# Turning the convolved blocks once into a staging tile and copying both halves from there, in a convolution and gated-projection kernel

## The chip, the cores and the metric

The kernel runs on one core of one Trainium2 chip. The metric is the device time of one launch in microseconds (us). The engines are named as the profile names them: PE (TensorE, matrix products; PEld is its loading of weights), DVE (VectorE), ACT (ScalarE), POOL (GpSimd) and SP (SyncE). SP computes nothing here. It issues nearly all transfers, in the order of the program, one after the other, and it stands at a semaphore when the next transfer in its order is not yet allowed.

## The reference

Rows of x (8 sequences of 4096 tokens, 192 channels, float32) pass through a causal convolution of 7 taps with softmax weights, one set for each of 8 heads of 24 channels. The result goes through a gated unit:

```python
w = softmax(weight, axis=-1)                       # 8 heads x 7 taps
out = np.einsum('hk,bskhg->bshg', w, x_unf)        # x_unf: the 7 latest tokens, by head
h = x @ w_in                                       # 32768 x 192 @ 192 x 2048
g = h * np.cos(h)
return g @ w_out                                   # 32768 x 2048 @ 2048 x 192
```

## The kernel before

**Units and tiles.** The 32768 tokens are cut into 32 units of U = 1024, each of two tiles of T = 512. For a tile, PE makes the first projection in 8 steps (`mm1`, line 509): a step takes 3 chunks of 64 channels for two groups of 128 output features, as 6 products of 64 rows by 512 tokens into one of three buffers `h` in PSUM. ACT makes the cosine (line 516), DVE multiplies (line 520) into `g`, and PE makes the second projection of the tile before it in 64 steps of two products (`mm2_step`, line 558). The two halves of PE's rows (0 to 63 and 64 to 127) work at the same time on different products, so the convolved and transposed input `cT` must stand in both halves: channels of a chunk on 64 partitions, tokens along them, and the same again on the other 64.

**Two ways to convolve.** From unit 4 (`FIRST_RAW`) on, a unit is convolved in two ways. Its first 336 tokens are 3 blocks of 112 (`NPB`, `OP`) that PE convolves with banded matrices (`conv_unit`, line 280). ACT casts the result to bfloat16 into `ct_buf` (line 297) and a transposing transfer of SP (`turn_unit`, line 320) turns it into `cT`. The other 688 tokens are the raw part, 6 blocks of 115 (`NRB`, `OR`, with an overlap `OVER` of 2): their cast input `xk` is turned by a transfer into `rT` (line 348), ACT and POOL multiply it by the taps (lines 362 and 371), POOL sums the products into a tile `ro` (lines 378, 379 and 381), and 4 transfers copy `ro` into `cT` (`spread_raw`, line 393), two for each half of the partitions. `ro` holds the first three raw blocks on its partitions 0 to 63 and the last three on 64 to 127.

**How the blocks come into both halves before.** `ct_buf` has 10 slots of 64 columns for each of the 3 chunks, 3 with blocks and 7 that stay zero. Two transposes (part 0 and part 1, shifted by one slot) each turn 15 groups of two slots, zero slots too, into `cT`, whose upper half is thereby one block behind the lower. The copies of `ro` then overwrite the zeros.

**The order of the work** is written out by hand: `PE_ORDER` and `ACT_ORDER` have one string for the first tile of a unit and one for the second (other strings serve the first six tiles and the last one). In `PE_ORDER`, `h0` to `h7` are steps of the first projection, `mN` are N steps of the second, `c1` and `c2` are the halves of the convolution, `p` marks the end of the second projection of the tile before, and `q` its middle. Letters with a unit number issue work on other engines: `X` and `x` the two transposes, `U` the copies of `ro`, `T` the transpose of the raw part, `L` the loads, `O` the output store, `K` POOL's cast, `R` and `S` POOL's products and sums. Each engine, SP included, does its own part of this list in order. `X+1` is for the unit that comes next.

**The turn.** At the middle of the second projection (32 steps into it, at `q`) the row halves change banks, and likewise between `c1` and `c2`. The change is ordered through SP: `Turn.mark` puts an empty instruction on SP that waits for the last product before the change, and the first product after it waits for that empty instruction (line 199). So these products can start only when SP has come that far in its list:

```python
def mark(self, *insts):
    self.nop = nc.sync.nop()
    for m in insts:
        tc.add_manual_dep(self.nop.ins, m.ins.name, sync_dep, reason="row halves on one bank")
def wait(self, *insts):
    for m in insts:
        tc.add_manual_dep(m.ins, self.nop.ins.name, sync_dep, reason="row halves on one bank")
```

Of the kernel before, what the change touches and what calls it, by code (L numbers as in the profile page):

```python
# [9 lines left out]
BF16 = mybir.dt.bfloat16  # L10
AF = mybir.ActivationFunctionType
ALU = mybir.AluOpType
# [4 lines left out]
def kernel(  # L17
# [8 lines left out]
    nc = tc.nc  # L26
    B, S, D = x.shape
    H, K = weight.shape
    Dff = moe_w_in.shape[1]
    G = D // H  # L30
    NTOK = B * S
    T = 512
    NT = NTOK // T
    NB = T // 128
    U = 1024
    NU = NTOK // U
    UB = U // 128
    UPS = S // U
    TPU = U // T
    NF = Dff // 128  # L40
    NP = NF // 2
    NC = D // 64
    R = G // NC
# [3 lines left out]
    FIRST_RAW = 4  # L47
    NPB, OP = 3, 112
    NRB = 6
    OR = -(-(U - NPB * OP) // NRB)  # L50
    OVER = NRB * OR - (U - NPB * OP)
    WN = NC * NRB // 2
# [2 lines left out]

    SLOTS = 10
    CW = SLOTS * OP

    xf = x.rearrange("b s d -> (b s) d")

    consts = ctx.enter_context(tc.tile_pool(name="consts", bufs=1))
# [3 lines left out]
    cT_pool = ctx.enter_context(tc.tile_pool(name="cT", bufs=2))  # L67
    xk_pool = ctx.enter_context(tc.tile_pool(name="xk", bufs=2))
    ro_pool = ctx.enter_context(tc.tile_pool(name="ro", bufs=2))
# [22 lines left out]
    def load_unit(u, n0=0, n1=UB, queue=nc.sync):  # L92
        if u >= FIRST_RAW:
            x_tiles[u] = xin.tile([128, UB + 1, D], FP32, name="x_f")

            raw, half = NPB * OP - OVER + OR - 128, NRB // 2
            for slots, t0, step in ((slice(NPB, UB + 1, 2), raw, OR), (slice(NPB + 1, UB + 1, 2), raw + half * OR, OR),
                                    (slice(0, NPB), OP - 128, OP)):
                rows = xf[u * U + t0 : u * U + t0 + 128, :]
                rows = bass.AP(rows.tensor, rows.offset, [[D, 128], [step * D, half if slots.step else NPB], [1, D]])  # L100
                queue.dma_start(out=x_tiles[u][:, slots, :], in_=rows)
            return
        if n0 == 0:
            x_tiles[u] = xin.tile([128, UB + 1, D], FP32, name="x_f")
        queue.dma_start(out=x_tiles[u][:, n0:n1, :],
                          in_=xf[u * U + n0 * 128 : u * U + n1 * 128, :].rearrange("(n p) d -> p n d", p=128))
# [3 lines left out]
    w = consts.tile([128, NC, NP, 128], BF16)  # L110
# [62 lines left out]
    nc.gpsimd.affine_select(out=ident, in_=ident, compare_op=ALU.not_equal, fill=1.0, base=0, pattern=[[1, 128]],  # L173
                            channel_multiplier=-1)
    wn = consts.tile([128, HQ, K], BF16)
    ct_bufs = [consts.tile([128, NC * SLOTS + 1, 64], BF16, name="ct_buf%d" % i) for i in range(2)]

    wmax = consts.tile([128, HQ, 1], FP32)
    nc.vector.tensor_reduce(out=wmax[:, :, 0], in_=w_bc, axis=mybir.AxisListType.X, op=ALU.max)
# [46 lines left out]
    have = {("whole", 0, 0)}  # L226
# [45 lines left out]
    def conv_unit(u, banks):  # L272


        ps = banks()
        sides = [slice(0, 64), slice(64, 128)]

        def mm(h, side):
            first, last = h % 4 == 0 and h // 4 == side, h % 4 == 3 and h // 4 != side
            return nc.tensor.matmul(  # L280
                out=ps[h // 4][:, 0 : NPB * 4 * G].rearrange("p (m i r) -> p i m r", m=NC * NPB, i=4)[:, h % 4],
                lhsT=band[sides[side], h, 128 - OP : 256 - OP], rhs=xk[u][sides[side], 0 : NC * NPB, R * h : R * (h + 1)],
                start=first, stop=last, skip_group_check=True)

        for h in range(4):
            ms = mm(h, 0), mm(h + 4, 1)
        turn = Turn()
        turn.mark(*ms)
        yield
        for h in range(4):  # L290
            ms = mm(h + 4, 0), mm(h, 1)
            if h == 0:
                turn.wait(*ms)
        yield
        for b in range(2):
            w0 = 4 * R * b
            nc.scalar.copy(ct_bufs[u % 2][0:OP, 0 : NC * SLOTS].rearrange("p (k n) m -> p k n m", k=NC)[:, :, 1 : NPB + 1, w0 : w0 + 4 * R],  # L297
                           ps[b][0:OP, 0 : NPB * 4 * G].rearrange("p (k n w) -> p k n w", k=NC, w=4 * R))
            if b:
                have.update((("conv", u, 0), ("conv", u, 1)))  # L300
            yield

    cT = {}

    def double_unit(u):

# [5 lines left out]
    def turn_unit(u, n0=0, n1=UB + 1, part=0):  # L312
        if u >= FIRST_RAW:
            assert {("conv", u, 0), ("conv", u, 1)} <= have
            if part == 0:
                cT[u] = cT_pool.tile([128, NC * (UB + 1) * 128], BF16, name="cT")
            else:
                have.update((("whole", u, 0), ("whole", u, 1)))
            to = cT[u][:, 0 : NC * CW].rearrange("p (n s t) -> p s n t", s=2, t=OP)
            nc.sync.dma_start_transpose(out=to[:, part],  # L320
                                        in_=ct_bufs[u % 2][0:OP, part : part + NC * SLOTS].rearrange("p s m -> p (s m)"))
            cT.pop(u - 2, None)
            return
        assert ("double", u) in have
        have.update((("turn", u), ("whole", u, 1)) if u == 0 else (("turn", u),))
        ct = ct_tiles.pop(u)
        if u not in cT:
            cT[u] = cT_pool.tile([128, NC * (UB + 1) * 128], BF16, name="cT")
        nc.sync.dma_start_transpose(out=cT[u].rearrange("p (s t) -> p s t", t=128)[:, NC * n0 : NC * n1],
                                    in_=ct[:, n0:n1].rearrange("p n c t k -> p (n c t k)"))  # L330
        cT.pop(u - 2, None)
# [8 lines left out]
            nc.tensor.matmul(out=ps, lhsT=pick[:, i].rearrange("p t q i r -> p (t q i r)"), rhs=wn[:, i, :],  # L340
                             start=i == 0, stop=i == 1, skip_group_check=True)

    rT, pa, ro = {}, {}, {}

    def turn_raw(u):

# [27 lines left out]
    def sum_raw(u):  # L374

        assert {("tap", u, j, PARTS[k].start) for j in range(PA) for k in "lr"} <= have
        a, p, add = pa.pop(u), raw_prod, nc.gpsimd.tensor_tensor
        add(out=p[:, 0:PA], in0=p[:, 0:PA], in1=a, op=ALU.add)  # L378
        add(out=p[:, 0:2], in0=p[:, 0:2], in1=p[:, 2:4], op=ALU.add)  # L379
        ro[u] = ro_pool.tile([128, WN, OR], BF16, name="ro")  # L380
        add(out=ro[u], in0=p[:, 0], in1=p[:, 1], op=ALU.add)  # L381

    def spread_raw(u):

        have.add(("raw", u))
        r = ro.pop(u).rearrange("p (k w) t -> p k (w t)", k=NC)
        run = NRB // 2 * OR
        for to, t0 in ((0, NPB * OP + OP), (1, NPB * OP)):
            for v in range(2):
                skip = 0 if v else OVER  # L390
                d = cT[u][64 * to : 64 * to + 64, t0 : t0 + (NC - 1) * CW + 2 * run - OVER]
                d = bass.AP(d.tensor, d.offset + v * (run - OVER), [d.ap[0], [CW, NC], [1, run - skip]])
                nc.sync.dma_start(out=d, in_=r[64 * v : 64 * v + 64, :, skip:])  # L393

    def mend_edges(u):

# [11 lines left out]
                            in1=wn.rearrange("p h (o k) -> p h o k", o=1).to_broadcast([128, HQ, E, K]), op=ALU.mult)  # L408
# [10 lines left out]
    for i, k in enumerate("DPDPDPDPDPDPDPAA"):  # L419
        q, rows = divmod(i, 4)  # L420
# [73 lines left out]
    def mm1(t, j, n0=0, n1=NB):  # L494

        assert ("whole", t // TPU, t % TPU) in have
        assert t < TPU * FIRST_RAW or ("raw", t // TPU) in have
        c = cT[t // TPU]
        h = h_pool.tile([128, 2, T], FP32, name="h")
        for k in range(NC):  # L500
            for i in range(2):
                rows = slice(64 * i, 64 * i + 64)
                if t >= TPU * FIRST_RAW:
                    t0 = k * CW + (t % TPU) * T + n0 * 128 + (0 if i else OP)
                    rhs = c[rows, t0 : t0 + (n1 - n0) * 128]
                else:
                    m = (t % TPU) * NB
                    rhs = c[rows].rearrange("p (n c k) -> p n c k", c=NC, k=128)[:, m + n0 : m + n1, k, :]
                nc.tensor.matmul(out=h[:, i, n0 * 128 : n1 * 128], lhsT=w[rows, k, j, :], rhs=rhs, start=(k == 0), stop=(k == NC - 1))  # L509
        return h  # L510
# [81 lines left out]

    PE_ORDER = ['m11 S+1 h0 m3 h1 m6 X+1 h2 m8 K+3 q h3 m6 h4 m18 h5 m8 p x+1 h6 h7 O m4', 'm11 h0 m6 h1 R+2 m5 h2 m6 q h3 m7 h4 m7 U+1 c1 m12 c2 h5 T+3 m6 p h6 L+4 O h7 m4']
    ACT_ORDER = ['s0 s1 a0l1 s2 s3 s4 Q a1l4 a1r4 V s5 s6 s7', 'a0r0 s0 s1 s2 s3 a2l3 s4 a2r4 ec1 Q ec2 s5 P s6 s7']

    PE_FIRST = ["K1 h0a h0b W0 h1 h2 h3 r h4 w5 d11 w4 h5 d21 W1 c11 X0 m1 h6 m11 h7 L2 c21 D1",
# [19 lines left out]
    for t in range(NT + 1):  # L618
# [34 lines left out]
        def of_unit(k, v):  # L653
            if (k, v) == ("K", 1):
                cast_unit(1, 0, NB)
                cast_unit(1, NB)
            elif k == "Z":
                nc.gpsimd.memset(ct_bufs[v][0:OP], 0.0)
            elif (k, v) == ("X", 0):
                turn_unit(0, NB, UB)  # L660
            elif k == "L":
                load_unit(v)
                if v < FIRST_RAW:
                    load_edges(v)
            else:
                {"K": cast_unit, "D": double_unit, "X": turn_unit, "Y": mend_edges, "T": turn_raw, "R": tap_raw, "S": sum_raw,
                 "U": spread_raw, "x": lambda u: turn_unit(u, part=1)}[k](v)
# [64 lines left out]
```

## Time and profile before

| what | value |
|---|---|
| median of 3 timed runs | 713.48 us (712.57 to 714.96) |
| the profiled execution, its own time | 710.59 us |
| span of the profiled execution | 708.8 us |
| PE busy | 695.2 us (98%) |
| DVE, ACT, POOL busy | 651.5, 644.5, 562.4 us |
| the transfers of SP's queue (q1) | 105 MB, 70.2% of 16 engines' span |

In the rows of the profile, `SPq` is SP's queue of instructions and L199 is the empty instruction of a turn. A row of a timeline gives the start, the duration, engine, line, operation, the tiles (out<-in) and how many instructions of the kind are merged in the row; a bracket behind it is idle time of that engine ahead of the row, with what ended it. For a transfer on SPq the duration is the time for which SP is held by issuing it, not the time until its data lands. A row of waits gives the total, the number of times and the longest.

### The profile page before, as it was taken

The page shows a single profiled execution, that of the slowest core. Times are in us where ns is not written, and L with a number is a line of the kernel's source. Part 1 is how long each engine was busy: PE and PEld are TensorE (multiplying, and loading weights), DVE is VectorE, ACT ScalarE, POOL GpSimd, SP SyncE. Part 2 cuts the span into 40 slices and gives each one's busy share as a digit, 9 for nine tenths or more (in the row PEclk, how much of TensorE's full clock was granted, in tenths as well). Part 3 has the DMA queues.
Part 4 walks back from the last instruction along what each step waited for, and adds up shares of the span by engine and source line. Part 5 has one row for each costly group of instructions (what it writes and reads, how often), then busy time and mean ns, then how long its engine had stood idle before and what let it go on. Part 6 is the DMA issues. An engine that isn't in the chain of part 4 may idle for free.

```text
span 708.8 us, 26916 instructions
## 1 busy us (share of the span) xinstructions
PE 695.2 (98%) x11828; PEld 505.3 (71%) x11830; DVE 651.5 (92%) x628; ACT 644.5 (91%) x801; POOL 562.4 (79%) x298
## 2 busy tenths in 40 slices
PE   8999999999999999999999999999999999999997
PEld 4677777777777676777777767777677776777776
DVE  6889999899999998999999998999989999999996
ACT  7889999999999999999999998999899999999875
POOL 6526888899888899888898887998888988887600
PEclk9999999999999999999999999999999999999999
DMA  8964786779985669977778765798877698665421
GB/s 213 254 148 97 161 156 160 111 170 174 169 182 151 116 162 180 171 165 125 157 156 190 170 149 121 157 173 169 170 133 154 152 184 169 160 120 109 96 76 47
DMA packets 239045, 107.66 MB, mean 152 GB/s; under 512 B 145488, under 2 KB 238544, under 8 KB 238928
## 3 DMA queue, kind: packets, MB, share of 16 engines
q1 hardware_dynamic: 238216, 104.97, 70.2%
q8 instruction: 92, 1.51, 0.9%
q0 software_dynamic: 416, 0.79, 0.8%
q14 instruction: 25, 0.20, 0.1%
q10 hardware_dynamic: 296, 0.20, 0.1%
HBM read 31.36 MB, written 25.17 MB: 80 GB/s over the span
## 4 chain that ended last, share of the span: by engine, by line
PE 95%; SPq 2%; DVE 1%; ACT 1%; issue 0%; POOL 0%; POOLq 0%
PE o_ps L558 47%; PE h L509 46%; PE h L280 1%; SPq L393 1%; SPq L320 1%; DVE g L520 0%; PE h L558 0%; ACT cs L516 0%; PE h L232 0%; DVE band L421 0%; ACT ct L478 0%; POOL mask L162 0%; ACT mask L167 0%; ACT ct L444 0%; DVE diag L410 0%
## 5 line engine op out<-in xcount | busy, mean ns | idle before, releaser
L520 DVE TENSOR_TENSOR g<-h,cs 128x1024 bf16<-128x1024 f32 (+1 forms) x513 | 597.7, 1215 | 25.5 <-ACT cs L516 17.9
L516 ACT ACTIVATE cs<-h 128x1024 bf16<-128x1024 f32 (+1 forms) x513 | 510.6, 1023 | 51.8 <-PE h L509 39.6
L558 PEld LDWEIGHTS <-g 64*128 64x128 bf16 x8192 | 352.7, 94 | 111.1 <-SPq L199 14.7
L558 PE MATMUL o_ps<-wo,g 64*128 64x192 bf16 x8128 | 413.7, 243 | 5.7 <-SPq L199 5.3
L509 PE MATMUL h<-cT,w 64*128 64x512 bf16 (+1 forms) x3078 | 405.8, 376 | 0.8 <-DVE g L520 0.5
L378 POOL TENSOR_TENSOR raw_prod<-raw_prod,pa 128x3105 f32<-128x3105 f32 x28 | 159.1, 5681 | 70.2 <-ACT pa L362 70.2
L509 PEld LDWEIGHTS <-w 64*128 64x128 bf16 x3078 | 143.5, 94 | 76.9 <-issue 2.1
L371 POOL TENSOR_SCALAR raw_prod<-rT,tap 128x1035 f32<-128x1035 bf16 x112 | 126.1, 1148 | 0.1
L362 ACT ACTIVATE pa<-rT,tap 128x575 f32<-128x575 bf16 (+1 forms) x168 | 118.9, 724 | 0.0
L379 POOL TENSOR_TENSOR raw_prod<-raw_prod 128x2070 f32<-128x2070 f32 x28 | 107.8, 3851 | 2.2
L214 POOL CAST xk<-x_f 128x1152 bf16<-128x1152 f32 (+1 forms) x56 | 75.1, 1374 | 0.0
L381 POOL TENSOR_TENSOR ro<-raw_prod 128x1035 bf16<-128x1035 f32 x28 | 66.8, 2387 | 2.2
L577 DVE COPY o_sb<-o_ps 128x384 f32<-128x384 f32 x92 | 48.5, 554 | 21.9 <-PE o_ps L558 21.8
L297 ACT CAST ct_buf<-h 112x288 bf16<-112x288 f32 x56 | 19.5, 402 | 1.1 <-PE h L280 1.0
L280 PE MATMUL h<-xk,band 64*128 64x72 bf16 x448 | 16.5, 194 | 0.9 <-SPq L199 0.9
L577 ACT COPY o_sb<-o_ps 128x384 f32<-128x384 f32 x34 | 16.0, 475 | 0.1
L280 PEld LDWEIGHTS <-band 64*128 64x128 bf16 x448 | 13.5, 95 | 1.6 <-SPq L199 1.6
L222 POOL CAST x_bf<-x_f 128x768 bf16<-128x768 f32 (+2 forms) x5 | 9.0, 1810 | 6.2 <-DMA x_f<-in_x_dram 6.2
L310 POOL COPY ct<-ct 128x1728 bf16<-128x1728 bf16 x3 | 4.9, 1630 | 10.3 <-ACT ct L242 10.3
L139 PE MATMUL o_ps<-zero 128*128 128x512 bf16 x20 | 7.2, 502 | 1.3 <-DVE zero L134 1.3
L400 POOL COPY cT<-cT 128x144 bf16<-128x144 bf16 x3 | 0.9, 306 | 8.9 <-DMA cT<-ct 8.9
L242 ACT CAST ct<-h 128x432 bf16<-128x432 f32 x12 | 5.9, 531 | 0.4 <-issue 0.4
(66 smaller groups left out, 52.3 us busy)
## 6 DMA issues: line engine op xcount, KB each, us to landing
x_f<-in_x_dram SPq DMA_DIRECT2D x84, 288.0 KB, 3.7
out_dram<-o_sb SPq DMA_DIRECT2D x63, 384.0 KB, 5.2
cT<-ro SPq DMA_DIRECT2D x56, 129.4 KB, 2.8
cT<-ro SPq DMA_DIRECT2D x56, 128.6 KB, 3.0
x_f<-in_x_dram SPq DMA_DIRECT2D x4, 384.0 KB, 5.8
g<-in_moe_w_out_dram SPq DMA_DIRECT2D x4, 384.0 KB, 7.8
x_f<-in_x_dram SPq DMA_DIRECT2D x2, 768.0 KB, 5.1
cT<-ct_buf SPq DMA_TRANSPOSE x56, 5.1
```

What stands on the lines that cost most here:

```text
L214: copy(out=xk[u][:, NC * n0 : NC * n1].rearrange("p (k n) m -> p k n m", k=NC), in_=x_tiles[u][:, n0:n1].rearrange("p n (m k) -> p k n m", ...
L280: return nc.tensor.matmul(out=ps[h // 4][:, 0 : NPB * 4 * G].rearrange("p (m i r) -> p i m r", m=NC * NPB, i=4)[:, h % 4], lhsT=band[sides ...
L362: nc.scalar.mul(pa[u][:, j, part], tap_window(u, j)[:, part], tap[:, j : j + 1])
L371: nc.gpsimd.tensor_scalar(out=p[:, j], in0=tap_window(u, PA + j), scalar1=tap[:, PA + j : PA + j + 1], scalar2=1.0, op0=ALU.mult, op1=ALU. ...
L378: add(out=p[:, 0:PA], in0=p[:, 0:PA], in1=a, op=ALU.add)
L379: add(out=p[:, 0:2], in0=p[:, 0:2], in1=p[:, 2:4], op=ALU.add)
L381: add(out=ro[u], in0=p[:, 0], in1=p[:, 1], op=ALU.add)
L509: nc.tensor.matmul(out=h[:, i, n0 * 128 : n1 * 128], lhsT=w[rows, k, j, :], rhs=rhs, start=(k == 0), stop=(k == NC - 1))
L516: nc.scalar.activation(out=cs[:, :, part], in_=h[:, :, part], func=AF.Sin, bias=math.pi / 2.0, scale=1.0)
L520: nc.vector.tensor_tensor(out=g_tiles[t][:, 2 * j : 2 * j + 2, part], in0=h[:, :, part], in1=cs[:, :, part], op=ALU.mult)
L558: ms.append(nc.tensor.matmul(out=o_ps[tt, b, si], lhsT=g_tiles[tt][rows, f, s * 128 : (s + 1) * 128], rhs=wo[rows, f // 2, f % 2, :], star ...
L577: (copy or copies[b])(o_sb[t][:, 2 * b : 2 * b + 2, :].rearrange("p s d -> p (s d)"), o_ps.pop((t, b)))
```

## The change

The two transposes no longer write `cT`. `ct_buf` loses its zero slots but for the first group: it has 12 slots, block 0 with a zero slot beside it for each chunk, then blocks 1 and 2 for each chunk. Each transpose turns 3 groups in place of 15, into columns 0 to 223 of a staging tile, in which POOL's last sum now writes the raw part behind them (columns 224 to 568). The unit's tokens are laid out anew: partitions 0 to 63 of the staging tile hold tokens 0 to 568 (blocks 0 and 1, then three raw blocks), partitions 64 to 127 hold block 2 and the other three raw blocks, tokens 569 to 1023 behind an overlap. Four transfers then copy these, 569 and 455 tokens long, into each half of `cT`, which has no pads any more and is the same in both halves. The loads of x follow the new order of blocks (1, 4 and 4 slots in place of 3, 3 and 3), and ACT's two casts take both banks at once, 384 and 192 elements in place of 288 and 288.

The written-out orders change too. In a unit's first tile `X+1` stands behind `q` and no longer ahead of it, `x+1` stands earlier, `S+1` later in the list; in the second tile `U+1` stands nearer to `q`; in both `O` stands ahead of `p`, so that it stores the output of one tile earlier. One tap product of ACT is moved behind the third cosine.

```diff
-    SLOTS = 10
-    CW = SLOTS * OP
+    NLO = 2
+    LO = NLO * OP + NRB // 2 * OR
+    STAGE = 16 * (-(-LO // 16))
+    SLOTS = 4 * NC
...
-            raw, half = NPB * OP - OVER + OR - 128, NRB // 2
-            for slots, t0, step in ((slice(NPB, UB + 1, 2), raw, OR), (slice(NPB + 1, UB + 1, 2), raw + half * OR, OR),
-                                    (slice(0, NPB), OP - 128, OP)):
+            for slots, t0, n in ((slice(0, 1), OP - 128, 1), (slice(1, UB + 1, 2), 2 * OP - 128, 1 + NRB // 2),
+                                 (slice(2, UB + 1, 2), LO - OVER + OP - 128, 1 + NRB // 2)):
...
-        for b in range(2):
-            w0 = 4 * R * b
-            nc.scalar.copy(ct_bufs[u % 2][0:OP, 0 : NC * SLOTS].rearrange("p (k n) m -> p k n m", k=NC)[:, :, 1 : NPB + 1, w0 : w0 + 4 * R],
-                           ps[b][0:OP, 0 : NPB * 4 * G].rearrange("p (k n w) -> p k n w", k=NC, w=4 * R))
+        both = ps[0].tensor, ps[0].offset, [ps[0].ap[0][0], OP]
+        for n0, n1 in ((1, NPB), (0, 1)):
+            to = ct_bufs[u % 2][0:OP, 2 * NC * min(n0, 1) : 2 * NC * (min(n0, 1) + 1)]
+            to = to.rearrange("p (k n) (b w) -> p b k n w", k=NC, b=2)[:, :, :, 0 : n1 - n0]
+            nc.scalar.copy(to, bass.AP(both[0], both[1] + 4 * R * n0, [both[2], [T, 2], [NPB * 4 * R, NC], [4 * R, n1 - n0], [1, 4 * R]]))
...
+    def stage_of(u):
+        if u not in stage:
+            stage[u] = ro_pool.tile([128, NC, STAGE], BF16, name="ro")
+        return stage[u]
...
-            to = cT[u][:, 0 : NC * CW].rearrange("p (n s t) -> p s n t", s=2, t=OP)
-            nc.sync.dma_start_transpose(out=to[:, part],
-                                        in_=ct_bufs[u % 2][0:OP, part : part + NC * SLOTS].rearrange("p s m -> p (s m)"))
+            nc.sync.dma_start_transpose(out=stage_of(u)[:, :, part * OP : (part + 1) * OP],
+                                        in_=ct_bufs[u % 2][0:OP, 2 * NC * part : 2 * NC * (part + 1)].rearrange("p s m -> p (s m)"))
...
-        ro[u] = ro_pool.tile([128, WN, OR], BF16, name="ro")
-        add(out=ro[u], in0=p[:, 0], in1=p[:, 1], op=ALU.add)
+        add(out=stage_of(u)[:, :, NLO * OP : LO], in0=p[:, 0].rearrange("p (k w) t -> p k (w t)", k=NC),
+            in1=p[:, 1].rearrange("p (k w) t -> p k (w t)", k=NC), op=ALU.add)
...
-        for to, t0 in ((0, NPB * OP + OP), (1, NPB * OP)):
-            for v in range(2):
-                skip = 0 if v else OVER
-                d = cT[u][64 * to : 64 * to + 64, t0 : t0 + (NC - 1) * CW + 2 * run - OVER]
-                d = bass.AP(d.tensor, d.offset + v * (run - OVER), [d.ap[0], [CW, NC], [1, run - skip]])
-                nc.sync.dma_start(out=d, in_=r[64 * v : 64 * v + 64, :, skip:])
+        for half in range(2):
+            rows = slice(64 * half, 64 * half + 64)
+            nc.sync.dma_start(out=to[rows, :, 0:LO], in_=r[0:64, :, 0:LO])
+            nc.sync.dma_start(out=to[rows, :, LO:U], in_=r[64:128, :, OP + OVER : LO])
...
-                    t0 = k * CW + (t % TPU) * T + n0 * 128 + (0 if i else OP)
+                    t0 = k * U + (t % TPU) * T + n0 * 128
...
-    PE_ORDER = ['m11 S+1 h0 m3 h1 m6 X+1 h2 m8 K+3 q h3 m6 h4 m18 h5 m8 p x+1 h6 h7 O m4', 'm11 h0 m6 h1 R+2 m5 h2 m6 q h3 m7 h4 m7 U+1 c1 m12 c2 h5 T+3 m6 p h6 L+4 O h7 m4']
-    ACT_ORDER = ['s0 s1 a0l1 s2 s3 s4 Q a1l4 a1r4 V s5 s6 s7', 'a0r0 s0 s1 s2 s3 a2l3 s4 a2r4 ec1 Q ec2 s5 P s6 s7']
+    PE_ORDER = ['m11 h0 m3 h1 S+1 m6 h2 m8 q X+1 h3 K+3 m6 h4 m17 h5 x+1 m9 O p h6 h7 m4', 'm11 h0 m5 h1 R+2 m7 h2 m5 q U+1 h3 m8 h4 m6 c1 m12 c2 T+3 h5 m6 O p L+4 h6 h7 m4']
+    ACT_ORDER = ['s0 s1 s2 a0l2 s3 s4 Q a1l4 a1r4 V s5 s6 s7', 'a0r0 s0 s1 s2 s3 a2l3 s4 a2r4 ec1 Q ec2 s5 P s6 s7']
...
-                nc.gpsimd.memset(ct_bufs[v][0:OP], 0.0)
+                nc.gpsimd.memset(ct_bufs[v][0:OP, 0 : 2 * NC], 0.0)
```

More of the change, by code (lines that the diff above doesn't have):

```diff
@@ L94, in load_unit @@
             x_tiles[u] = xin.tile([128, UB + 1, D], FP32, name="x_f")
-            raw, half = NPB * OP - OVER + OR - 128, NRB // 2
-            for slots, t0, step in ((slice(NPB, UB + 1, 2), raw, OR), (slice(NPB + 1, UB + 1, 2), raw + half * OR, OR),
-                                    (slice(0, NPB), OP - 128, OP)):
+            for slots, t0, n in ((slice(0, 1), OP - 128, 1), (slice(1, UB + 1, 2), 2 * OP - 128, 1 + NRB // 2),
+                                 (slice(2, UB + 1, 2), LO - OVER + OP - 128, 1 + NRB // 2)):
                 rows = xf[u * U + t0 : u * U + t0 + 128, :]
-                rows = bass.AP(rows.tensor, rows.offset, [[D, 128], [step * D, half if slots.step else NPB], [1, D]])
+                rows = bass.AP(rows.tensor, rows.offset, [[D, 128], [OR * D, n], [1, D]])
                 queue.dma_start(out=x_tiles[u][:, slots, :], in_=rows)
@@ L175 @@
     wn = consts.tile([128, HQ, K], BF16)
-    ct_bufs = [consts.tile([128, NC * SLOTS + 1, 64], BF16, name="ct_buf%d" % i) for i in range(2)]
+    ct_bufs = [consts.tile([128, SLOTS, 64], BF16, name="ct_buf%d" % i) for i in range(2)]
     wmax = consts.tile([128, HQ, 1], FP32)
@@ L294, in conv_unit @@
         yield
-        for b in range(2):
-            w0 = 4 * R * b
-            nc.scalar.copy(ct_bufs[u % 2][0:OP, 0 : NC * SLOTS].rearrange("p (k n) m -> p k n m", k=NC)[:, :, 1 : NPB + 1, w0 : w0 + 4 * R],
-                           ps[b][0:OP, 0 : NPB * 4 * G].rearrange("p (k n w) -> p k n w", k=NC, w=4 * R))
-            if b:
+        both = ps[0].tensor, ps[0].offset, [ps[0].ap[0][0], OP]
[3 more added lines that the diff above has]
+            nc.scalar.copy(to, bass.AP(both[0], both[1] + 4 * R * n0, [both[2], [T, 2], [NPB * 4 * R, NC], [4 * R, n1 - n0], [1, 4 * R]]))
+            if n0 == 0:
                 have.update((("conv", u, 0), ("conv", u, 1)))
             yield
-    cT = {}
+    cT, stage = {}, {}
+    def stage_of(u):
+        if u not in stage:
+            stage[u] = ro_pool.tile([128, NC, STAGE], BF16, name="ro")
+        return stage[u]
     def double_unit(u):
@@ L314, in turn_unit @@
             assert {("conv", u, 0), ("conv", u, 1)} <= have
[L315 to L318, printed above, removed]
-            to = cT[u][:, 0 : NC * CW].rearrange("p (n s t) -> p s n t", s=2, t=OP)
-            nc.sync.dma_start_transpose(out=to[:, part],
-                                        in_=ct_bufs[u % 2][0:OP, part : part + NC * SLOTS].rearrange("p s m -> p (s m)"))
-            cT.pop(u - 2, None)
+            have.add(("turned", u, part))
+            nc.sync.dma_start_transpose(out=stage_of(u)[:, :, part * OP : (part + 1) * OP],
+                                        in_=ct_bufs[u % 2][0:OP, 2 * NC * part : 2 * NC * (part + 1)].rearrange("p s m -> p (s m)"))
             return
@@ L341, in spread_taps @@
                              start=i == 0, stop=i == 1, skip_group_check=True)
-    rT, pa, ro = {}, {}, {}
+    rT, pa = {}, {}
     def turn_raw(u):
@@ L379, in sum_raw @@
         add(out=p[:, 0:2], in0=p[:, 0:2], in1=p[:, 2:4], op=ALU.add)
-        ro[u] = ro_pool.tile([128, WN, OR], BF16, name="ro")
-        add(out=ro[u], in0=p[:, 0], in1=p[:, 1], op=ALU.add)
+        have.add(("summed", u))
+        add(out=stage_of(u)[:, :, NLO * OP : LO], in0=p[:, 0].rearrange("p (k w) t -> p k (w t)", k=NC),
+            in1=p[:, 1].rearrange("p (k w) t -> p k (w t)", k=NC), op=ALU.add)
     def spread_raw(u):
-        have.add(("raw", u))
-        r = ro.pop(u).rearrange("p (k w) t -> p k (w t)", k=NC)
-        run = NRB // 2 * OR
-        for to, t0 in ((0, NPB * OP + OP), (1, NPB * OP)):
-            for v in range(2):
-                skip = 0 if v else OVER
-                d = cT[u][64 * to : 64 * to + 64, t0 : t0 + (NC - 1) * CW + 2 * run - OVER]
-                d = bass.AP(d.tensor, d.offset + v * (run - OVER), [d.ap[0], [CW, NC], [1, run - skip]])
-                nc.sync.dma_start(out=d, in_=r[64 * v : 64 * v + 64, :, skip:])
+        assert {("turned", u, 0), ("turned", u, 1), ("summed", u)} <= have
+        have.update((("whole", u, 0), ("whole", u, 1)))
+        cT.pop(u - 2, None)
+        cT[u] = cT_pool.tile([128, NC * (UB + 1) * 128], BF16, name="cT")
+        to, r = cT[u][:, 0 : NC * U].rearrange("p (k t) -> p k t", k=NC), stage.pop(u)
+        for half in range(2):
+            rows = slice(64 * half, 64 * half + 64)
+            nc.sync.dma_start(out=to[rows, :, 0:LO], in_=r[0:64, :, 0:LO])
+            nc.sync.dma_start(out=to[rows, :, LO:U], in_=r[64:128, :, OP + OVER : LO])
     def mend_edges(u):
@@ L496, in mm1 @@
         assert ("whole", t // TPU, t % TPU) in have
-        assert t < TPU * FIRST_RAW or ("raw", t // TPU) in have
         c = cT[t // TPU]
```

## The prediction

> **What bounds the kernel now.** I read the page first: the busy shares and the chain that ended last.
>
> ```profile
> span 708.8 us, 26916 instructions
> ...
> PE 695.2 (98%) x11828; PEld 505.3 (71%) x11830; DVE 651.5 (92%) x628; ACT 644.5 (91%) x801; POOL 562.4 (79%) x298
> ...
> PE 95%; SPq 2%; DVE 1%; ACT 1%; issue 0%; POOL 0%; POOLq 0%
> ```
>
> PE sets the time, and the only other part of the chain that is worth anything is 2% of SP's queue. So the question is not how much transfer work the change saves but whether PE ever stands because of it. The waits, longest in total first, give the sizes:
>
> ```profile
> PEld L558 <- SPq L199: 14.7, 24, 1.6
> ...
> PE o_ps L558 <- SPq L199: 5.3, 7, 1.1
> ...
> PEld L280 <- SPq L199: 1.6, 3, 0.9
> ...
> PE h L509 <- DVE g L520: 0.5, 2, 0.4
> ```
>
> PE stands for the empty instruction of a turn (L199), 24 times before the second projection and 3 times before the second half of the convolution, and hardly for anything else. Weight loads run ahead of products, so 14.7 us is no loss of time by itself. For that I compare whole units, each from its raw copies to the next, in windows: the columns are the length, busy time by engine (and instructions), the granted clock, the transfer share and GB/s.
>
> ```profile
> core 0: us, PE busy (x) PEld busy (x) DVE busy (x) ACT busy (x) POOL busy (x), PEclk, DMA share, GB/s
> 344.30:365.48 21.18, 21.18 (x372) 15.58 (x369) 20.14 (x20) 20.12 (x26) 19.04 (x10) 1.00 0.80 162
> 365.48:386.66 21.18, 21.18 (x372) 15.58 (x369) 20.14 (x20) 20.12 (x26) 19.03 (x10) 1.00 0.71 161
> 408.56:431.20 22.64, 21.53 (x372) 15.45 (x369) 20.23 (x20) 20.24 (x26) 19.75 (x10) 1.00 0.71 151
> ```
>
> A quiet unit takes 21.18 us with PE busy all of it at full clock, two in a row to the hundredth. That is the floor: the change leaves the number of PE's instructions in a unit alone, and in such a unit DVE, ACT and POOL still have 1 us to spare. The third unit, with the same 372 products, took 1.46 us more. SP's and PEld's timelines of it say why:
>
> ```profile
> 417.17 1.32 SPq L348 DMA_TRANSPOSE rT<-xk  x1
> 418.54 1.66 SPq L101 DMA_DIRECT2D x_f<-in_x_dram  x3
> 420.31 0.42 SPq L580 DMA_DIRECT2D out_dram<-o_sb  x1
> 420.83 7.15 SPq L320 DMA_TRANSPOSE cT<-ct_buf  x2
> ...
> L320 SPq DMA_TRANSPOSE cT<-ct_buf x2: 1797/3514/5231, 420.8 to 426.2; - x2
> ...
> 424.19 0.40 PEld L509 LDWEIGHTS <-w 64*128 64x128 bf16 x6
> 426.17 0.44 PEld L558 LDWEIGHTS <-g 64*128 64x128 bf16 x12 [1.58 <-SPq L199]
> ```
>
> The row that begins with L320 is minimum, median and maximum in ns of the two transposes of this window. The first held SP for 5.23 us, from 420.83 to 426.06; the empty instruction of the turn at `q` stands behind it in SP's list, and 0.11 us later PE's weights moved on, after 1.58 us. PE stood because SP was still issuing a transpose, not because data was missing.
>
> How much is that over the run? The copies of `cT<-ro` follow a turn at once and so mark each unit:
>
> ```profile
> L393 SPq DMA_DIRECT2D cT<-ro x112: 593/611/1885, 91.5 to 674.6; - x112
> ...
> DMA to landing us min/median/max: 2.5/3.0/4.2
> ```
>
> 112 copies are 28 units of four. The fourth of a unit starts some 1.95 us behind the first (three issues of 0.61 with their gaps), so the first copies of units 1 and 28 lie 674.6 - 1.95 - 91.5 = 581.15 us apart, 27 units, 21.52 us each. At the floor they would take 27 x 21.18 = 571.9. **The whole loss in the steady part is 9.3 us**, and 1.6 of it is put down to the convolution's turn (the row PEld L280), which leaves 7.7 us for the turn at `q`.
>
> **The change part by part.** A quiet unit shows where each thing would now stand:
>
> ```profile
> 356.78 5.11 SPq L320 DMA_TRANSPOSE cT<-ct_buf  x2
> ...
> 362.95 2.40 POOL L381 TENSOR_TENSOR ro<-raw_prod 128x1035 bf16<-128x1035 f32 x1
> ...
> 370.67 2.59 SPq L393 DMA_DIRECT2D cT<-ro  x4
> ...
> 372.72 0.29 PE L280 MATMUL h<-xk,band 64*128 64x72 bf16 x8
> ...
> 373.44 1.34 SPq L348 DMA_TRANSPOSE rT<-xk  x1
> ...
> 373.76 0.25 PEld L280 LDWEIGHTS <-band 64*128 64x128 bf16 x8
> ...
> 374.19 0.70 ACT L297 CAST ct_buf<-h 112x288 bf16<-112x288 f32 x2
> ...
> 374.82 1.66 SPq L101 DMA_DIRECT2D x_f<-in_x_dram  x3
> ...
> 376.59 0.42 SPq L580 DMA_DIRECT2D out_dram<-o_sb  x1
> ...
> 377.65 0.59 PE L509 MATMUL h<-cT,w 64*128 64x512 bf16 x4
> ...
> 381.53 0.54 PEld L558 LDWEIGHTS <-g 64*128 64x128 bf16 x12 [0.22 <-SPq L199]
> ...
> 391.84 0.63 SPq L393 DMA_DIRECT2D cT<-ro  x1
> ```
>
> *The transposes* go from 15 groups to 3 each and, more important, `X+1` moves behind the turn at `q`. SP then has, between the raw copies and that turn, only the raw transpose (1.34), a store (0.42, of an output one tile older, for which it no longer waits) and the loads (1.66): done at about 373.4 + 3.5 = 376.9, where the turn needs it near 381.3 (PEld's row at 381.53, less its wait of 0.22). That leaves some 4.4 us of empty list ahead of it. So the 7.7 us go whatever a short transpose costs to issue. Behind the turn, `X`, `x` and a store have until the copies at 391.84. A transpose of 3 groups costs between a third of the raw one's 1.34 (9 groups; 0.45) and, if the size did not matter, the 5.23 above: two of these and a store end at 381.3 + 10.9 = 392.2, just where it would begin to matter. I take the low end, since the raw row is the nearest in size, and 0 on the path.
>
> *What is late next?* The copies wait for both transposes. These land 3.9 to 8.4 us after issue now:
>
> ```profile
> DMA to landing us min/median/max: 3.9/5.1/8.4
> ```
>
> Issued by 382.2, the second lands by 390.6 at the worst, ahead of 391.84. POOL's last sum ended at 362.95 + 2.40 = 365.35 for the copies at 370.67; moving `S+1` down the list does not move it among POOL's own work, and its strided output could double its 2.40 unseen. ACT's casts keep 576 elements and the 0.70; their end at 374.9 is 6 us ahead of the moved transpose. The moved tap product and the shifts by a step of `m` change no count; DVE and ACT have 1 us a unit to take them up. Each at 0.
>
> *The copies grow.* Four of 64 x 3 runs of 345 or 343 elements become runs of 569 and 455. Worked out from these sizes that is 2 x (213 + 171) = 768 KB a unit for 516.
>
> ```profile
> x_f<-in_x_dram SPq DMA_DIRECT2D x84, 288.0 KB, 3.7
> ...
> cT<-ro SPq DMA_DIRECT2D x56, 129.4 KB, 2.8
> cT<-ro SPq DMA_DIRECT2D x56, 128.6 KB, 3.0
> ```
>
> A load of 159 KB more takes 0.7 to 0.9 us more to land, about 5 ns a KB, so 252 KB more are at most 1.3 us if the four queue behind each other, and 0 if the 0.65 us between issues hides it. I take 1.0, since 200 KB at 5 ns is more than that spacing. The fourth is issued 1.95 us after 370.67 and lands, at 3.0, at 375.6; the next unit's first product starts at 377.65. The slack is 2.0 us, 1.0 after the change. The latest copies (4.2 in place of 3.0) would be 0.2 us too late with that growth and 1.2 + 1.3 - 2.0 = 0.5 with the most. I take 0, since the median is far from it; the bound is 0.5 us in a bad third of the units, 9 of them, some 4 us.
>
> *The convolution's turn* stays behind the four copies in SP's list (moving `U+1` nearer to `q` changes nothing: it follows the same turn). It fails when an issue takes long, as here:
>
> ```profile
> 263.53 3.85 SPq L393 DMA_DIRECT2D cT<-ro  x4
> ...
> 267.50 0.18 PEld L280 LDWEIGHTS <-band 64*128 64x128 bf16 x8 [0.85 <-SPq L199]
> ```
>
> The issue of 4 copies took 3.85 in place of 2.59 and PE lost 0.85. The loads of 288 KB are issued in 1.66 for three, less than the copies' 0.6 each, so issue time does not follow size, and I leave these 1.6 us as they are; bounds 0 and twice that.
>
> *The end:* the last stretch issues two stores where there was one, some 5 us ahead of the last products; 0 to 0.5 us.
>
> **Sum.** The profiled execution took 710.59. 710.59 - 7.7 = 702.9. The median of the timed runs is 713.48, 2.9 above it. If those 2.9 are more of the same stops, the new median is 703; if they lie outside, 705.8. Stops differ from unit to unit and the timed runs spread over 2.4 us, so I lean to the first: **704.0 us**.
>
> The Trainium skill speaks against this: "DMA: Bandwidth & Descriptors", section "Issuing engines are not separate DMA queues", says that the time a sequencer takes to initiate a transfer is usually small beside the transfer. By that rule nothing is to be had at SP, and the sum is 713 (rival C). The trace disagrees: the transpose that held SP for 5.23 us belongs to a kind that lands in 3.9 to 8.4.
>
> **Rivals.**
> *A, forecast (0.70).* The stops at `q` go, the rest stays: 701 to 706.
> *B (0.13).* They go, but late copies (up to 4 us) or longer holds at the convolution's turn (up to 1.6 more) take part of it back: 706 to 711.
> *C (0.07).* The change does not do what it says for PE: SP is as late at the turns as before, because backlog of the queue and not the transposes held it, and a load or store is held in their place. For it: even 3 loads took 1.66 to issue right ahead of the long hold. Against: 4.4 us of empty list. 713.
> *D, slower (0.10).* The next unit's first product waits for the copies in every unit. For it: the copies are the only transfer with a deadline as near as 2.0 us, and they grow by half. It decides once the growth costs over 2.0 us. At twice my upper bound, 2.6, each of 28 units loses 0.6: 17 us, against 7.7 gained: 713.5 - 7.7 + 17 = 723. Against: the load rows give 1.3 at most.
>
> The Trainium skill has a rule that bears on D: "DMA: Bandwidth & Descriptors", "Rules for kernel authors", says that two transfers to disjoint partition halves serialize and should be one. By it the four copies queue and the growth is the full 1.3 us; no run here shows it yet.
>
> **How the numbers follow.** About 0.3% (2.1 us) is what a measurement of this kernel can tell from no change, so faster means under 711.3. A and B are faster (0.83), C the same (0.07), D slower (0.10). A and B hold 0.83, so the range runs from 700.5 (710.59 - 9.3 = 701.3 with every stop gone, and a little) to 711.
>
> **What would show it.** In the profile after: units of 21.18 us throughout; the wait of PEld L558 for the empty instruction down from 24 times to a few; the transposes held well under 1 us and the first of them behind the turn; the copies' landing at 3.5 to 4.5. A wait of PE's first projection for a transfer into `cT` in each unit would mean D; waits at the turn at `q` as long as before would mean C.

## The result, and the profile after

The changed kernel took 702.12 us, the median of 4 runs (701.73 to 702.68), beside 713.15 us (712.57 to 714.96) for the kernel before: a ratio of 0.9842, 95% interval 0.9822 to 0.9861. The forecast was 704.0 in a range of 700.5 to 711.0. The profiled execution took 701.73 us, of which 699.9 is the span.

The page of the kernel after: its span, the busy shares, SP's queue of transfers, and the chain that ended last.

```profile
span 699.9 us, 26863 instructions
...
PE 692.3 (99%) x11828; PEld 516.1 (74%) x11830; DVE 650.9 (93%) x628; ACT 644.4 (92%) x801; POOL 559.9 (80%) x298
...
q1 hardware_dynamic: 162952, 92.93, 57.3%
...
PE 96%; DMA 1%; POOL 1%; DVE 0%; SPq 0%; issue 0%; ACT 0%; POOLq 0%
```

PE, DVE, ACT and POOL have the busy time that they had, within 3 us, and SP's queue went from 2% of the chain to nothing. The empty instruction of the turns (now L200) shows where it went:

```profile
L200 SPq EVENT_SEMAPHORE  x94: 17/17/17, 25.4 to 694.4; - x94
...
who waited for it (us, times):
  PEld L281: 0.4, 1
```

There are 94 turns as before. Weights waited for one of them, once, where they had waited 24 times at the second projection and 3 times at the convolution. Four units in a row, as windows:

```profile
core 0: us, PE busy (x) PEld busy (x) DVE busy (x) ACT busy (x) POOL busy (x), PEclk, DMA share, GB/s
324.65:345.83 21.18, 21.18 (x370) 16.28 (x368) 20.14 (x20) 20.12 (x26) 19.03 (x10) 1.00 0.65 140
345.83:367.01 21.18, 21.18 (x370) 16.28 (x368) 20.14 (x20) 20.12 (x26) 19.02 (x10) 1.00 0.61 141
367.01:388.19 21.18, 21.18 (x370) 16.28 (x368) 20.14 (x20) 20.13 (x26) 18.98 (x11) 1.00 0.57 140
388.19:409.67 21.48, 21.35 (x370) 15.60 (x368) 20.12 (x20) 20.23 (x26) 19.64 (x10) 1.00 0.56 138
```

Three are at the floor of 21.18 that the quiet units of before had. The fourth holds the run's one wait of note, 0.35 us at the convolution's turn. The timeline of SP in the third window is what the prediction laid out from rows of before:

```profile
367.01 0.61 SPq L395 DMA_DIRECT2D cT<-ro  x1
367.67 0.60 SPq L396 DMA_DIRECT2D cT<-ro  x1
368.32 0.61 SPq L395 DMA_DIRECT2D cT<-ro  x1
368.98 0.62 SPq L396 DMA_DIRECT2D cT<-ro  x1
369.77 1.54 SPq L350 DMA_TRANSPOSE rT<-xk  x1
371.36 1.03 SPq L582 DMA_DIRECT2D out_dram<-o_sb  x1
372.44 2.06 SPq L102 DMA_DIRECT2D x_f<-in_x_dram  x3
377.69 2.49 SPq L323 DMA_TRANSPOSE ro<-ct_buf  x2
380.31 0.51 SPq L582 DMA_DIRECT2D out_dram<-o_sb  x1
```

After the loads, SP is through at 374.5 and stands idle until the turn at `q` has passed; the two transposes start behind it, at 377.69, and the next thing that PE needs of SP is the turn just ahead of the copies at 388.19.

### The profile page after: what moved, and what is told of

It reads as the page before. It is cut to its first block, busy times and chain, and to the rows that moved or that the text cites. A ratio compares the mean times of both kernels' runs of the same rounds, so it can differ in the third digit from the quotient of the medians.

```text
span 699.9 us, 26863 instructions
## 1 busy us (share of the span) xinstructions
PE 692.3 (99%) x11828; PEld 516.1 (74%) x11830; DVE 650.9 (93%) x628; ACT 644.4 (92%) x801; POOL 559.9 (80%) x298
## 4 chain that ended last, share of the span: by engine, by line
PE 96%; DMA 1%; POOL 1%; DVE 0%; SPq 0%; issue 0%; ACT 0%; POOLq 0%
PE o_ps L560 48%; PE h L511 47%; PE h L281 1%; DMA x_f<-in_x_dram 1%; POOL x_bf L223 0%; PE h L560 0%; PE h L233 0%; SPq L395 0%; DVE g L522 0%; SPq L396 0%; ACT cs L518 0%; POOL mask L163 0%; PE o_ps L140 0%; ACT mask L168 0%; DVE diag L413 0%
## 5 line engine op out<-in xcount | busy, mean ns | idle before, releaser
L518 ACT ACTIVATE cs<-h 128x1024 bf16<-128x1024 f32 (+1 forms) x513 | 510.8, 1023 | 44.0 <-PE h L511 36.5
L560 PEld LDWEIGHTS <-g 64*128 64x128 bf16 x8192 | 359.6, 94 | 96.5 <-issue 0.7
L511 PEld LDWEIGHTS <-w 64*128 64x128 bf16 x3078 | 150.4, 94 | 72.9 <-issue 2.2
L300 ACT CAST ct_buf<-h 112x384 bf16<-112x384 f32 (+1 forms) x56 | 19.5, 403 | 0.2 <-PE h L281 0.2
L403 POOL COPY cT<-cT 128x144 bf16<-128x144 bf16 x3 | 0.9, 306 | 11.6 <-DMA cT<-ct 11.6
```

Of the source, the lines that this page charges most:

```text
L518: nc.scalar.activation(out=cs[:, :, part], in_=h[:, :, part], func=AF.Sin, bias=math.pi / 2.0, scale=1.0)
L560: ms.append(nc.tensor.matmul(out=o_ps[tt, b, si], lhsT=g_tiles[tt][rows, f, s * 128 : (s + 1) * 128], rhs=wo[rows, f // 2, f % 2, :], star ...
```

## The experiments

Two explanations were set against each other. **Place in SP's list:** PE lost time only because SP was held by issuing transfers just ahead of a turn. **Transfer load:** it was the amount of transfer work that had to fall.

### One letter moved in the kernel before

```diff
-'m11 S+1 h0 m3 h1 m6 X+1 h2 m8 K+3 q h3 m6 ...
+'m11 S+1 h0 m3 h1 m6 h2 m8 K+3 q X+1 h3 m6 ...
```

> The kernel before with one letter moved: X+1 (the first transpose, still 15 groups) behind the turn at q. Theory 'place in SP's list': the 7.7 us of stops at q go, the 1.6 us at the convolution's turn stay: profiled 702.9, 703 to 705 timed, with no wait of PEld L558 for L199. Rival 'transfer load': the long transposes keep the queue full (70% of 16 engines), so something else holds SP: 709 to 713. Risk that both share: the second transpose now lands close to the raw copies, which wait for it, by up to 0.5 us a unit.

703.35 us (703.30 to 703.53), ratio 0.9863 (0.9835 to 0.9892). Its groups of waits and its transposes:

```profile
PEld L280 <- SPq L199: 2.1, 3, 0.8
...
PE h L280 <- SPq L199: 1.5, 3, 0.6
L320 SPq DMA_TRANSPOSE cT<-ct_buf x56: 1388/1780/3685, 81.1 to 656.3; - x56
```

No wait at `q` is left, with all 105 MB of transfers still there (69.0% of the engines' span). The 3 stops at the convolution's turn stayed, as expected. The transposes, still of 15 groups, now held SP for 1.78 us in the median, against 2.77 before: behind the turn, nothing was issued just ahead of them. One moved letter gives 9.2 us (712.57 for the kernel before on that chip, less 703.35), where the whole change gave 11.0.

### The orders alone

The kernel before with both order strings of the kernel after and no other edit.

> The kernel before with both order strings of the kernel after and nothing else: two transposes of 15 groups into cT, small raw copies, but X behind the turn and stores and loads moved. Theory 'place in SP's list': 702 to 704.5, no wait at the turn of q. Rival 'transfer load': 708 to 713.

704.73 us (703.74 to 704.92), ratio 0.9879 (0.9850 to 0.9909); no wait at `q`, 4 at the convolution's turn (2.5 us). That is 0.2 us above what was expected. The other moves in the orders bring nothing beyond that one letter; the median even lies 1.4 us above that run's, for which no run gives the cause.

### The staging alone

The kernel after with both order strings of the kernel before, so that the short transposes stand ahead of the turn.

> The kernel after with both order strings of the kernel before: short transposes and larger copies, but X ahead of the turn. Theory 'place in SP's list' says that a short hold fits ahead of the turn too: X can start at about 6.4 us behind the raw copies, the turn is needed 10.6 us behind them, and two transposes hold SP 1.25 us each, so no stop: 701.5 to 703. Rival 'order': any transpose ahead of the turn stops PE: 707 to 712. Rival 'transfer load': 702.

702.12 us (701.85 to 702.98), ratio 0.9850 (0.9815 to 0.9884). Its transposes and its one kind of wait of weights for a turn:

```profile
L323 SPq DMA_TRANSPOSE ro<-ct_buf x56: 1175/1476/2977, 76.2 to 653.7; - x56
PEld L281 <- SPq L200: 0.7, 2, 0.4
```

So it is not the order either. At this place in the list, behind loads and a store, the first transpose of a unit held SP for 1.6 us in the median (3.0 at the most) and fits ahead of the turn; with 15 groups, in the kernel before, it held SP there for 4.0 in the median (5.2 at the most) and does not. Either half of the change removes the stops at `q`, and both together do no more than the staging alone. The runs with the large transposes stay 1.2 to 2.6 us above those with the staging, and their profiles put 2.1 and 2.5 us of waits at the convolution's turn against 0.4 and 0.7. That fits a small part for the transfer load there, through now and then a longer issue of a copy; it was not tried by itself.

These longer issues are not spread at random. With the staging alone, and in both profiles of the kernel after, they fall in the units 7, 15 and 23, every eighth. They go with the packets of the queue that the profile calls instruction (number, MB, share of 16 engines; from the page of the kernel after):

```profile
q8 instruction: 92, 1.51, 0.9%
```

These are 92 packets of 16 KB, one about every 7.5 us. In the traces of all runs, the fourth and fifth issues of the two runs with a large fifth transfer (below) left aside, 49 copies took more than 0.85 us to issue. For each of the 49 such a packet started between 0.7 us before and 0.25 us after the start of the issue; of the 1155 other copies only 58 had one as near. No run moved these packets, so this is a coincidence in time and not a cause that was tried, and why the stops are longer with the large transposes stays open.

### The copies issued earlier

```diff
-'m11 h0 m5 h1 R+2 m7 h2 m5 q U+1 h3 ...
+'m11 h0 m5 U+1 h1 R+2 m7 h2 m5 q h3 ...
```

> The kernel after with U+1 moved ahead of the turn at q in a unit's second tile (behind h0 m5), so that SP issues the four copies some 4 us earlier and no longer between the two turns. Theory: all data for them is there, the one wait left at the convolution's turn (0.4 us) goes, and the next unit's first product has 4 us more to spare: equal to the kernel after or up to 0.5 us faster, 701.3 to 702.2. Rival 'copies are late' (part of the time of the kernel after is products waiting for copies): faster by 2 us or more.

701.18 us (701.11 to 701.37), ratio 0.9833 (0.9805 to 0.9861), just under what was expected, and no turn waited for at all. Long issues are still there, of up to 2.2 us for one copy, but at this place PE does not wait for them. A second time it ran beside the kernel after on one chip:

> The kernel after, unchanged, beside the next one on the same chip: 701.7 to 702.7.

> The kernel after with U+1 ahead of the turn at q, unchanged from its first run: 701.1 to 701.4 and 0.5 to 1.0 us under the kernel after, since the kernel after still stops now and then at the convolution's turn. If both lie within their spread, the earlier copies are worth nothing that can be told.

702.41 us for the kernel after (701.85 to 703.11; ratio 0.9855, 0.9833 to 0.9878) and 701.24 for this one (701.21 to 701.29; ratio 0.9839, 0.9817 to 0.9860). The two do not overlap: 1.2 us, 0.2%. It is the fastest version of this study, and its runs lie within 0.1 us here and 0.3 the first time, where the kernel after spreads over 1.3. That fits the stops being what makes its runs differ. A gain of 2 us or more, by which products would have been waiting for late copies, did not appear.

### A fifth transfer, in two places

```diff
+        for i in range(1):
+            nc.sync.dma_start(out=spare[u % 2][64 * i : 64 * i + 64, :, 0:LO], in_=r[0:64, :, 0:LO])
         for half in range(2):
```

> The kernel after with a fifth transfer ahead of the four raw copies of each unit: the same 213 KB into a spare tile that nothing reads. It asks how near the place of the copies is to costing time. Place in SP's list: the five hold SP some 3.25 us in place of 2.6, so the convolution's turn, which had about 0.5 us to spare, stops PE by 0.1 to 0.2 us in every unit: 705 to 708. Landing (rival D of the prediction): the two copies that the next unit's first product needs land 0.65 to 1.0 us later, about 5.2 to 6.4 us behind the first issue against the 6.97 where it starts: no wait but in a few units. If landing decides, the wait shows at the first projection's products for a transfer into cT, not at the turn.

727.29 us (726.72 to 727.92), ratio 1.0206 (1.0164 to 1.0247): in direction as expected, but 25 us in place of 3 to 6. The waits, and SP's and PEld's timelines in one unit:

```profile
PEld L281 <- SPq L200: 26.9, 27, 1.4
...
PE h L281 <- SPq L200: 20.9, 27, 1.2
...
357.02 0.61 SPq L395 DMA_DIRECT2D spare<-ro  x1
357.73 0.60 SPq L398 DMA_DIRECT2D cT<-ro  x1
358.38 0.61 SPq L399 DMA_DIRECT2D cT<-ro  x1
359.05 1.23 SPq L398 DMA_DIRECT2D cT<-ro  x1
360.32 0.65 SPq L399 DMA_DIRECT2D cT<-ro  x1
...
361.08 0.18 PEld L281 LDWEIGHTS <-band 64*128 64x128 bf16 x8 [0.94 <-SPq L200]
```

PE stopped at the convolution's turn in nearly every unit and never for data in `cT`. The expectation took each issue at 0.65; the fourth in a row takes twice that here, so that the five hold SP for 3.95 us, from 357.02 to 360.97 (the next expectation but one puts this at 3.7).

> The same fifth transfer, in the variant whose copies are issued ahead of the turn at q (U+1 behind h0 m5). Place in SP's list: SP has the time there, so the same extra work costs nothing: 701 to 702. If the amount of transfer work counts, it is slower than that variant by as much as the fifth transfer cost in the other place.

701.33 us (701.18 to 701.50), ratio 0.9842 (0.9809 to 0.9875). The same five transfers, with the same long fourth issue, stand 4 us earlier in SP's list, and they cost nothing:

```profile
361.55 0.61 SPq L395 DMA_DIRECT2D spare<-ro  x1
362.29 0.59 SPq L398 DMA_DIRECT2D cT<-ro  x1
362.92 0.61 SPq L399 DMA_DIRECT2D cT<-ro  x1
363.57 1.14 SPq L398 DMA_DIRECT2D cT<-ro  x1
364.76 0.63 SPq L399 DMA_DIRECT2D cT<-ro  x1
369.23 1.35 SPq L351 DMA_TRANSPOSE rT<-xk  x1
```

Between 365.4 and 369.2 SP stands waiting: there is the time that they used. This pair is the plainest answer to the two explanations, since the work is equal and only its place differs, by 26 us.

Why is the fourth issue long? The fifth transfer was cut to runs of 32 elements:

```diff
-out=spare[u % 2][64 * i : 64 * i + 64, :, 0:LO], in_=r[0:64, :, 0:LO]
+out=spare[u % 2][64 * i : 64 * i + 64, :, 0:32], in_=r[0:64, :, 0:32]
```

> As the run with a fifth transfer ahead of the four, with the fifth cut from runs of 569 elements to runs of 32 (12 KB in place of 213, the same 192 runs). There the fourth issue of each unit held SP 1.2 us in place of 0.6, the five took 3.7, and PE stopped 0.8 to 0.9 us at the convolution's turn in each unit. Theory 'backlog by data': SP is held because the data ahead of it has not been moved; with 12 KB the five take 3.25 us and the stop is some 0.2 us a unit: 704 to 710. Rival 'backlog by number': the fourth transfer in a row is held whatever its size: 725 to 729.

714.01 us (713.24 to 714.89, 10 runs), ratio 1.0007 (0.9989 to 1.0025). This falls between the two expectations, so SP's timeline decides, shown behind the wait for the turn:

```profile
PEld L281 <- SPq L200: 13.7, 27, 1.2
...
350.69 0.62 SPq L395 DMA_DIRECT2D spare<-ro  x1
351.47 0.60 SPq L398 DMA_DIRECT2D cT<-ro  x1
352.12 0.60 SPq L399 DMA_DIRECT2D cT<-ro  x1
352.77 0.62 SPq L398 DMA_DIRECT2D cT<-ro  x1
353.43 0.66 SPq L399 DMA_DIRECT2D cT<-ro  x1
```

The fourth issue is back at 0.62, behind as many transfers and runs: its hold goes with the size of the transfers ahead and not with the number issued. The small transfer, which lands in 1.9 us where the large one took 3.1, has also left the queue when the fourth is issued 2.1 us behind it, but the number in flight alone does not hold SP either: in the kernel after the fourth copy, of 171 KB, is issued with three in flight and took 0.62.

The time came out above 710 because the five held SP for 3.40 us, with a longer gap behind the first, and not 3.25, and because some units were held longer still. From one unit's first transfer to the next, 21 of 27 units lost 0.29 us against 21.18, in the median, at a hold of 3.41; the other six, each with a copy of 0.98 us or more, lost 0.6 to 1.2 at holds of 3.7 to 4.3. In the run with the large fifth transfer the quiet units lost 0.93 at 3.95. Both say that a unit loses what the hold has above 3.0 to 3.1 us. The kernel after, with 2.6, has about 0.5 to spare, as had been taken, and its two units that lost time at this turn lost 0.10 and 0.30 at holds of 3.14 and 3.35.

## Why the prediction was right, point by point

**The bound and the floor.** Units of 21.18 us with PE busy throughout were taken as what is left without stops. The kernel after has them nearly throughout: its first copies start at 91.7 and its last unit's third copy at 665.3, as the row says.

```profile
L395 SPq DMA_DIRECT2D cT<-ro x56: 602/611/1364, 91.7 to 665.3; - x56
...
DMA to landing us min/median/max: 3.3/4.1/5.4
L396 SPq DMA_DIRECT2D cT<-ro x56: 596/610/723, 92.4 to 665.9; - x56
...
DMA to landing us min/median/max: 3.5/4.5/6.4
```

A third copy starts 1.31 behind the first, so 27 units took 665.3 - 1.3 - 91.7 = 572.3 us, against 571.9 at the floor and 581.15 before. Of the 9.3 us that stops cost, 0.4 is left.

**The term for `q` (7.7 us)** went entirely, and for the reason given. Ahead of the turn SP had some 3 us of empty list (374.5 to 377.69 above) and not 4.4, since the store and the loads held it longer than in the rows of before. The prediction named the moved transpose as the more important part; the runs show that short transposes in the old place do it as well, so "more important" was not borne out.

**The term for the convolution's turn (1.6 us, left as it was)** is the one that was mis-sized: 0.4 stayed in this execution, and 0.7 in the profile of the kernel after run again. Together that is 7.7 + 1.2 = 8.9, and the profiled times differ by 710.59 - 701.73 = 8.9.

**From the profiled time to the median.** The 2.9 us by which the timed runs of before lay above the profiled one were taken, by choice, as more of the same stops. The kernel after has its median 0.4 us above its profiled time, and the version with no stop repeats to 0.3 us or better, which bears the choice out. With it and the term above, 702 was to be had in place of 704.

**The transposes' hold** was put at 0.45 us, from the raw transpose by its groups. Two took 2.49 us in the timeline above, 1.25 each, so that sign of the prediction, "well under 1 us", did not come. That is hardly less than the 1.39 of the shortest with 15 groups: the number of groups does not scale the hold where nothing was issued just ahead, while behind loads and a store it made the difference of 1.6 to 4.0 us. In its place the hold cost nothing.

**The copies' growth.** The landing went from 3.0 to 4.1 and 4.5 us, up to 1.5, a little over the bound of 1.3. It still made no wait, with more room than was worked out: a unit's first products read tokens 0 to 511, for which the two copies of 569 suffice. The second of them, issued 1.31 us behind the first and landing in 4.1, is there at 5.4 (6.7 at the longest, 5.4), and the first product starts 6.98 behind the first copy (377.65 less 370.67 in the prediction's rows, and nothing ahead of it was added). The trace bears this out: the third copy landed 5.5 us behind the first issue in the median, the fourth 7.0 and once 8.3, which is behind the start of the first product, and no product waited for it. By the third copy, which landed at 4.3 in the kernel before, the margin of rival D was 2.7 us ahead of the change and not 2.0, and 1.5 behind it.

**The Trainium skill's rules.** One engine stood for what the issuing sequencer had not yet reached, and the pair with the fifth transfer prices that at 26 us for equal transfers. The Trainium skill, "DMA: Bandwidth & Descriptors", section "Issuing engines are not separate DMA queues", says that the time to initiate a transfer is usually small beside the transfer; the trace agrees for a copy (0.61 us to issue, 4.1 to land) and not for a transpose of 15 groups behind loads and a store (up to 5.2 to issue, 3.9 to 8.4 to land).

The four copies queue behind each other: they are issued 0.65 us apart and land 3.3, 4.3, 5.5 and 7.0 us behind the first issue, 1.1 to 1.5 apart, and the 171 KB copy took longer than the 213 KB one, 4.5 against 4.1. The Trainium skill, "DMA: Bandwidth & Descriptors", section "Rules for kernel authors", says that two transfers to disjoint partition halves serialize; the trace agrees.

**Rivals.** B's and C's signs (longer holds at the convolution's turn; waits at `q` as before) and D's (a wait for a transfer into `cT` in each unit) are absent from the profile after. B's mechanism is real and near: 0.8 us more of SP's time between the two turns cost 11.6 us in the run with the small fifth transfer (714.01 less 702.41 on the same chip).

## What to carry to other kernels

Where an in-order issuing queue also carries the semaphores that order the busiest engine, its list has deadlines: ask of each transfer issued ahead of such a point how long its issue can hold the queue at that place, behind what was issued just before, and not only how much it moves. Compare units of the same work in the trace; if the quiet ones repeat to the hundredth, the sum over the others is all that can be gained, and a profile of two neighbours shows what it hangs on. Before rebuilding the data path, try to move the transfer behind the point: here one letter in the order gave over 80% of the gain.

## What was not expected of the hardware

The time for which a transfer holds SP was the same 0.61 us for copies of 129, 171 and 213 KB and 0.62 for 12 KB, but 1.2 us for the fourth in a row when the three ahead of it had 597 KB and it was itself one of 213; with 12 KB for one of the three it was 0.62 again. In the kernel after, a fourth of 171 KB behind the same 597 KB took 0.62. With its own size counted, the queued data was 811 KB where the hold came and 768 KB where it did not; no run looked for where between these, or by what else, it begins. A transpose of 15 groups held SP for 1.78 us in the median behind the turn and up to 5.2 right behind loads and a store.
